# Half of x transposed on VectorE and moved inside SBUF, instead of on TensorE

## The chip, the core and the metric

The kernel runs on one core of a Trainium2 chip. A core has five engines with their own instruction streams: TensorE (PE in the profile, with PEld for its weight loads), VectorE (DVE), ScalarE (ACT), GpSimd (POOL) and SyncE (SP). SP only issues transfers here; ACT and POOL can issue transfers too. Engines work out of SBUF (128 partitions), matmuls write into PSUM (8 banks), and 16 transfer engines move data between device memory (DRAM) and SBUF or inside SBUF. The metric is device time of one execution in microseconds (us).

## The reference: what is computed

The input x is 2048 rows (positions) of 512 features, in bf16. Two branches are computed from it and mixed by a gate per row:

```python
g = sigmoid((x * gate_w).sum(-1, keepdims=True))
X = rfft2(x) * (w_r + 1j * w_i);  a = irfft2(X)            # spectral branch
h = x @ w1 + b1;  act = h * tanh(softplus(h));  b = act @ w2   # dense branch, 512 -> 1792 -> 512
out = g * a + (1 - g) * b
```

## The kernel before, in words

**Data.** x lies in SBUF as 16 tiles `xo[:, t, :]` of 128 rows by 512 features. Both branches need the features on the partitions, so x is also kept transposed, as `xT`: four groups `q` of 128 features by 2048 rows. A row tile `t` is 128 columns of it. Even and odd features are separated, which is why the transposes read with a step of two elements.

**Transposes.** The loop at L466 makes ten groups of TensorE transposes, `tr0a` to `tr14` (L476, 64 matmuls of 128 columns, two tiles per full group), each followed by an eviction `evx` from PSUM to `xT` by VectorE (L404, 1024 elements per partition for a full group; ScalarE may take the four half groups).

**Spectral branch.** The sequence of 2048 positions is split into 16 by 128, and the transforms are matmuls with small tables. In order:
- For each quarter `h` of the rows, VectorE forms the sum `ts` and the difference `td` of the two halves of the features in `xT` (L497, helper line L409). Steps `a1` (L512) transform them, ScalarE copies one part (`eg`, L519) and VectorE combines (`e1p`, `e1m`, `e1f`).
- `s1` (L538) transforms the other axis, `e2` evicts, and SP writes 16 pieces to a DRAM scratch (`r1w`, L546). When all are there, four transfers read them back in another order (`r1r`, L619).
- `s2` (L635) completes the forward transform with the table `RF` (`ld_rf`). VectorE multiplies with the filters W (`wm`, 16 instructions, helper line L409), GpSimd combines the products (`wz`, 16 instructions). The edge columns of W are handled apart: `wcols` (GpSimd), `rcw` (TensorE, L584 and L585), `weff` (VectorE), `wab1` and `wab2` (GpSimd, L598 to L605), and small steps `cv`, `crv`, `cm`, `chs`, `wc` per pair.
- `s2i` (L695) begins the inverse transform; `e4` evicts, and a second exchange through DRAM follows (`r2w`, `r2r`).
- For each row tile: `s1i` (L723), eviction `e5`, `a1i` (L734), `gc` on ScalarE, `sam` and `sap` on VectorE (L745, both scale by the gate), `sbm` and `sbp` on GpSimd (three of the 32 on VectorE; L751, helper line L409), which give the spectral share in `ga`.

**Dense branch.** In four quarters `c` of 512 rows: `mm1` (L773, 14 groups of four matmuls with 512 columns; the first four groups of the first quarter are cut into halves), `mish` on ScalarE (L788) into `act[:, c % 3]`, and `mm2` (L803, per row tile two half groups of seven matmuls). The result is scaled by 1 - g in `bev` (L755 on ScalarE or L756 on VectorE), and `sum` on VectorE (helper line L409) adds the spectral share in `xo`. The last two tiles take one instruction `fin` (L815) in place of both. SP stores pairs of tiles.

**Gate.** `gdot` (L554, VectorE) is one dot product per tile; `gpow` (L559, GpSimd) and three small VectorE steps give g and 1 - g. In the kernel before, the dot products 8 to 15 come after the last `e1`.

**Order.** Every engine and queue runs its list strictly in order. The lists come from one string, `ORDER` (L258): it names all steps in one sequence, with the engine where there is a choice and the PSUM bank. Waits between engines are semaphores derived from what each step reads and writes. So a step that is late holds up everything behind it in its own engine's list.

SP's list begins with the loads of x, part of w1 and the tables FM and GM, then `ld_gw`, 18 loads of W, `ld_rf`, both halves of w2, then the 16 writes `r1w`, the reads `r1r` and `ld_ri`. Three loads of w1 are on ACT's queue. GpSimd issues one small transfer, `ld_b1`.

Of the kernel before, what the change touches and what calls it, by code (L numbers as in the profile page):

```python
# [13 lines left out]
NT = 16  # L14
# [151 lines left out]
class _Graph:  # L166
# [92 lines left out]
    "0M0N0U047050P060O07080Q2z09000S0A010R0B0C0D0T020E0F030V0G0H0W0I0J0X0x60z50Y0yv0Z0K10v1146v212v1H30a1366l51I6q0"  # L259
    "14v0L7011Jv6m6n6w1Kv0b716o0c726p731L40d1M36r1N0e1W50f6s6t741Ov1V70g1560h1Pv1X6x0i6y6u16v7510j1Qa1Zv6z0k1701av1"  # L260
    "971Yv77318v761R41Av781B61Sv7920l0m0n7B01fv7A0o7D10p7C1gv0q1D70r1Cv7E1h30s1r42j1s61j7F20t21v0u1Ev7H00v22v1i17G1"
    "T7J31kv7I1U1lv2451F27K7L01mv1t1Gv2371uv7N47M1vv252Ov7O7b127v1wa2D37c2k28a26v7d07f22Nv7e2l1b67g1n42m2E11ca7h22F"
    "7j01d1ov1e7i1x62Hv7k1p342922Gv1ya1q7l52Av2Ia2Q41z2P17m2Z67n0202n2R2b2B2J22Tv7o2a72C2Sv7p12Ka2Uv2cv7r67q2dv2L2V"
    "27s2M2ev7t02Wv2f67u7v12o2X2ga2p7x52Y7w2h2q7z07y2i2r816802s8F1822t3578H48G362u398J28I373A8L58K2v3B8N63C388M0w8P"
    "18O2w8R28Q2x8T02y8S3D4308U3E63Mv8V38X13Nv8W8Y3Rv3Pg313F7P03G323Qv3Og7Q333H3Tg3Z33Sg7Ra3a13b8Z63iv3I57S08a3mv3J"
    "3jv7T3K3L3U3nv3kg3V47Ua7V33c3Xa3Wv3d3pg3Y3e03v43f3og3w644v7W3lg3x3y49v7Y13g7Xv3z3h3q45v7Z48v46g4028307aa4147g3"
    "r4843ta4Bg3sv4Ag3u4H485a4I24Qv86642434J4K4C4Uv4L874Rv89188a4Vv4Sg4D44Wg4M38b24Ea4N4Fa4Tg8c8A4G4Xg8d74O8Ba4P4Y8"
    "C08e4Z28f14av4ba8D8g4c8t18Ev8v28u8x08w4d8z18y4e9124f904g933929549497096992989B79A4h39C4p59D04qv4ia4x64r59E4yv4"
    "j75534s5D45L156a5Ev5T04z65Ma8h24u504t4k5Uv4wg5N14m5F34vg525V55O8i4l9fv5G5Q4ng515b78k04og8jv5W5P54g5I5Sg5H5768l"
    "5ca9ev5853g9g599F75Rg5A8mv5Kg9H49G5Y5Cg5d65X9J09I9hv5e9lv5j45r39K5Jg8n75sv5ka5Bg9kv5g5z35ag9m6745f5l568a5t19iv"  # L270
    "8o60v5m5hg9j5u5o5ig5v6908pa6F45n5Zg6135w8q26Ga5qg629nv6A645pg8r6B9ov635xg9p6C6N46V59qv6Oa9L78sv5yg6Wa66g6P69rv"
    "6X46Q6H26Eg6d09s6Y9M6S6I6Dg6R6ea6K65g6J9O19Nv6Ug6a6Mg6Z9P9uv9tv6cv9v6f56Tg9Qa9R46bv6g9xv6h6Lg9S6i9wv6kv9y9V06j"
    "g9T9U9Y29W9b79X9Z9a9c9d"
)
NBF = 14
GD_N = 8
# [15 lines left out]
def _build(nc, A_x, A_w_r, A_w_i, B_x, B_w1, B_b1, B_w2, gate_w, out):  # L292
# [8 lines left out]
    with es:  # L301
# [4 lines left out]
        xT = sb("xT", [128, 4, NT * 128], BF)  # L306
# [42 lines left out]
        junk = Tg[:, 6144:6656]  # L349
# [4 lines left out]
        psf = ps[:].rearrange("p b x -> p (b x)")  # L354

# [110 lines left out]
        for t0, h in ((0, 0), (0, 1), (2, 0), (2, 1), (4, None), (6, None), (8, None), (10, None), (12, None), (14, None)):  # L466
# [4 lines left out]
            def f_tr(e, t0=t0, c0=c0, nc_=nc_, pt=pt):  # L471
                ins = None
                for i in range(2):
# [6 lines left out]
            evict(f"evx{t0}" + ("" if h is None else "ab"[h]), 256 * nc_, lambda t0=t0, c0=c0, nc_=nc_: xT[:, c0:c0 + nc_, 128 * t0:128 * (t0 + 2)],  # L480
                  lambda pt=pt, nc_=nc_: psb[:, pt.bank, 0:256 * nc_].rearrange("p (c j) -> p c j", c=nc_), rate=2.0,
                  reads=[("ptr", t0, h)], writes=[("xT", t0 + i, q) for i in range(2) for q in hs], frees=[pt], engs=("dve",) if h is None else ("dve", "act"))
        pb = _Ps(SPEC[::-1])
# [7 lines left out]
        for t in range(NT):  # L491
            if t % 4 == 0:
                G.cur_prio = PR["sp"] + 0.9
                h = t // 4
                cols = slice(512 * h, 512 * h + 512)
                for (nm, o, op) in (("s", 0, ALU.add), ("d", 2, ALU.subtract)):
                    tt(f"t{nm}{h}", lambda o=o, hb=h % 2: Tb[:, hb, o:o + 2, :], lambda cols=cols: xT[:, 0:2, cols],  # L497
                       lambda cols=cols: xT[:, 2:4, cols], op, 1024, rate=2.0,
                       reads=[("xT", 4 * h + i, q) for i in range(4) for q in range(2)], writes=[("T", h % 2, nm)])
            if t % 2 == 0:  # L500
# [3 lines left out]
                for half in range(2):  # L504
# [11 lines left out]
                    pe(f"a1{half}_{t}", 4 * mm(128), f_a1, reads=[("T", hb, "s"), ("T", hb, "d"), "FD"], writes=[("pa", t, half)], alloc=pa,  # L516
# [34 lines left out]
        for t in range(NT):  # L551
            G.cur_prio = PR["gate"] if t >= GD_N else 60.0
            G.add(f"gdot{t}", "dve", dve_dur(512),
                  lambda e, t=t: e.scalar_tensor_tensor(out=junk, in0=xo[:, t, :], scalar=1.0, in1=gwb,  # L554
                                                        op0=ALU.mult, op1=ALU.mult, accum_out=gdot[:, t:t + 1]),
                  reads=[("x", t), "gw"], writes=[("gd", t), "junk"], lock=True, deps=e1s[14] if t >= GD_N else ())

# [206 lines left out]
        for c in range(NCH):  # L764
            hb = c % 3
            G.cur_prio = PR["mm1"] - c
            for ft in range(NFT):
                pd = _Ps(DENSE[c])

                def f_mm1(e, c=c, ft=ft, pd=pd, cols=(0, 512), ks=range(4)):  # L770
                    ins = None
                    for i in ks:
                        ins = e.matmul(ps[:, pd.bank, cols[0]:cols[1]], w1_sb[:, i, 128 * ft:128 * (ft + 1)], xT[:, i, 512 * c + cols[0]:512 * c + cols[1]],  # L773
# [10 lines left out]
                else:  # L784
                    pe(f"mm1_{c}_{ft}", 4 * mm(512), f_mm1, reads=[("xT", 4 * c + i, q) for i in range(4) for q in range(2)] + [("w1", ft, 0), ("w1", ft, 1)],
                       writes=[("pm", c, ft)], alloc=pd, deps=mm2s.get(c - 3, ()), prio=pr_m)
                G.add(f"mish_{c}_{ft}", "act", act_dur(512, True),
                      lambda e, ft=ft, pd=pd, hb=hb: e.activation(act[:, hb, ft, :], ps[:, pd.bank, :], AF.Mish, bias=b1f[:, ft:ft + 1]),  # L788
                      reads=[("pm", c, ft), "b1f"], writes=[("act", hb, ft)], frees=[pd], prio=PR["mish"])
# [148 lines left out]
```

## Time and profile before

| | |
|---|---|
| Median of 3 runs | 130.04 us (129.64 to 130.09) |
| Span of the profiled execution | 128.0 us |
| The same less the median | -2.04 us |
| PE busy | 124.4 us (97%) |
| DVE busy | 92.2 us (72%) |
| ACT busy | 68.9 us (54%) |
| POOL busy | 54.4 us (42%) |
| Chain that ended last, by engine | PE 94%, transfers 3% |
| Moved | 20.11 MB, mean 157 GB/s |

The profile shows one execution; its own time is known only as its span, from the first to the last instruction. Lines are those of the kernel before (L773 is line 773); where a helper records an operation, its line stands for several steps. In a row of the costliest groups, the last number is the idle time of the engine just before these instructions, with what ended most of it. In the chain, each piece has a start, a length and what worked in it. A row of transfers gives the median time from issue to landing.

### The profile page before, as it was taken

To read this page: it belongs to the slowest core of one execution; us is meant where nothing else is said; L and a number is where in the kernel's file an instruction comes from. 1 tells how busy PE (TensorE), PEld (TensorE's weight loads), DVE (VectorE), ACT (ScalarE), POOL (GpSimd) and SP (SyncE) were. 2 spreads that over 40 slices of the span, in tenths; PEclk is the share of its full clock that TensorE was granted. 3 is DMA by queue.
4 is the path that set the end of the run, shared out by engine and by line. 5 is a ranking of instruction groups with operands and counts; after the bars stand their busy time and mean duration, and the time that the engine had idled before them with its cause. 6 is when DMAs were issued, how large, how long until landed. Compare 5 with 4: busy or idle time off the path is not lost.

```text
span 128.0 us, 2725 instructions
## 1 busy us (share of the span) xinstructions
PE 124.4 (97%) x1046; PEld 67.9 (53%) x1046; DVE 92.2 (72%) x176; ACT 68.9 (54%) x113; POOL 54.4 (42%) x82
## 2 busy tenths in 40 slices
PE   7899999999999999999999999999999999999992
PEld 5698566545444444444444444444674457464482
DVE  0359997999989929998957900500399799999872
ACT  1339377889978784224024274487873475462300
POOL 4000000001000996979688394000038986998120
DMA  3999999999976398002304105449600204022231
GB/s 76 346 390 394 303 185 185 173 272 354 334 235 202 99 384 356 0 0 61 108 0 133 38 0 164 133 104 351 239 0 5 82 0 164 3 87 82 82 123 41
DMA packets 18653, 20.11 MB, mean 157 GB/s; under 512 B 1488, under 2 KB 15696, under 8 KB 18512
## 3 DMA queue, kind: packets, MB, share of 16 engines
q1 hardware_dynamic: 17792, 19.15, 49.7%
q10 hardware_dynamic: 816, 0.79, 1.9%
q8 instruction: 8, 0.13, 0.5%
q14 instruction: 5, 0.04, 0.1%
q0 software_dynamic: 32, 0.00, 0.0%
HBM read 13.64 MB, written 6.29 MB: 156 GB/s over the span
## 4 chain that ended last, share of the span: by engine, by line
PE 94%; DMA 3%; SPq 0%; DVE 0%; issue 0%
PE ps L803 38%; PE ps L773 38%; DMA xo<-in_A_x_dram 3%; PE ps L734 3%; PE ps L723 3%; PE ps L512 3%; PE ps L538 3%; PE ps L476 3%; PE ps L695 2%; PE ps L635 2%; SPq L374 0%; DVE xo L815 0%; PE ps L652 0%; PE ps L484 0%; PE ps L425 0%
## 5 line engine op out<-in xcount | busy, mean ns | idle before, releaser
L773 PE MATMUL ps<-xT,w_sb 128*128 128x512 bf16 (+1 forms) x240 | 52.9, 365 | 0.0
L803 PE MATMUL ps<-w_sb,act 128*128 128x512 bf16 (+2 forms) x252 | 51.6, 355 | 0.0
L788 ACT ACTIVATE act<-ps,b1f 128x512 bf16<-128x512 f32 x56 | 38.4, 688 | 18.5 <-PE ps L773 17.3
L803 PEld LDWEIGHTS ps<-w_sb,act 128*128 128x128 bf16 x252 | 22.7, 98 | 22.3 <-issue 0.8
L773 PEld LDWEIGHTS ps<-xT,w_sb 128*128 128x128 bf16 x240 | 22.3, 98 | 21.2 <-issue 0.6
L409 POOL TENSOR_TENSOR Tg<-Qb 128x256 bf16<-128x256 f32 x29 | 22.1, 790 | 21.9 <-DVE Qb L745 21.8
L409 POOL TENSOR_TENSOR Zb<-Qb 128x510 bf16<-128x510 f32 x16 | 19.8, 1268 | 5.1 <-DVE Qb L409 5.0
L409 DVE TENSOR_TENSOR Qb<-ps,WT 128x1024 f32<-128x1024 f32 x16 | 18.8, 1213 | 3.4 <-PE ps L635 3.4
L755 ACT ACTIVATE xo<-ps,omg 128x512 bf16<-128x512 f32 x8 | 5.5, 687 | 18.4 <-PE ps L803 10.1
L745 DVE SCALAR_TENSOR_TENSOR Qb<-ps,gcol,Qb 128x256 f32<-128x256 f32 x32 | 13.7, 475 | 1.5 <-ACT Qb L739 1.0
L404 DVE CAST Ybuf<-ps 128x1024 bf16<-128x1024 f32 x7 | 8.6, 1222 | 7.1 <-PE ps L695 6.7
L409 DVE TENSOR_TENSOR Abuf<-ps,Tg 128x512 bf16<-128x512 f32 x16 | 10.4, 685 | 2.4 <-PE ps L512 2.1
L576 POOL COPY wrv<-WT 128x32 bf16<-128x32 bf16 x2 | 0.4, 223 | 26.1 <-DMA WT<-in_A_w_i_dram 26.1
L405 ACT ACTIVATE Ybuf<-ps 128x1024 bf16<-128x1024 f32 x9 | 9.1, 1021 | 4.3 <-PE ps L695 4.3
L554 DVE SCALAR_TENSOR_TENSOR Tg<-xo,Tg 128x512 bf16<-128x512 bf16 x16 | 11.0, 688 | 0.3
L404 DVE CAST Zb<-ps 128x512 bf16<-128x512 f32 x6 | 4.1, 687 | 8.9 <-PE ps L723 8.9
L404 DVE COPY xT<-ps 128x1024 bf16<-128x1024 bf16 (+1 forms) x10 | 5.6, 579 | 5.4 <-PE ps L476 5.4
L409 DVE TENSOR_TENSOR xo<-xo,Tg 128x512 bf16<-128x512 bf16 x14 | 8.5, 615 | 0.3 <-ACT xo L755 0.3
L739 ACT ACTIVATE Qb<-ps,gcol 128x256 f32<-128x256 f32 x16 | 7.0, 475 | 2.7 <-PE ps L734 1.6
L405 ACT ACTIVATE Zb<-ps 128x512 bf16<-128x512 f32 x10 | 5.7, 596 | 4.6 <-PE ps L723 3.2
L598 POOL TENSOR_TENSOR ch<-wq 128x32 f32<-128x32 f32 x1 | 0.6, 624 | 12.5 <-DVE wq L593 12.5
L476 PE MATMUL ps<-ident,xo 128*128 128x128 bf16 x64 | 5.1, 225 | 0.5 <-DMA xo<-in_A_x_dram 0.5
(59 smaller groups left out, 92.8 us busy)
## 6 DMA issues: line engine op xcount, KB each, us to landing
Abuf<-scr SPq DMA_DIRECT2D x8, 512.0 KB, 5.4
scr<-Ybuf SPq DMA_DIRECT2D x16, 128.0 KB, 3.9
scr<-Ybuf SPq DMA_DIRECT2D x4, 512.0 KB, 3.8
w_sb<-in_B_w_dram SPq DMA_DIRECT2D x2, 896.0 KB, 13.6
out_dram<-xo SPq DMA_DIRECT2D x7, 256.0 KB, 2.0
xo<-in_A_x_dram SPq DMA_DIRECT2D x3, 512.0 KB, 7.7
rt<-c_rt SPq DMA_DIRECT2D x2, 512.0 KB, 8.5
WT<-in_A_w_r_dram SPq DMA_DIRECT2D x7, 128.5 KB, 10.4
```

What stands on the lines that cost most here:

```text
L404: fs = {"dve": ("dve", dve_dur(n, rate=rate), lambda e: e.tensor_copy(out=dst(), in_=src())), "act": ("act", act_dur(n), lambda e: e.activ ...
L405: "act": ("act", act_dur(n), lambda e: e.activation(dst(), src(), AF.Copy))}
L409: f = lambda e: e.tensor_tensor(out=o(), in0=i0(), in1=i1(), op=op)
L476: ins = e.transpose(psb[:, pt.bank, o:o + 128], xo[:, t0 + i, d0:d0 + 255:2], ident[:, :])
L512: ins = e.matmul(ps[:, pa.bank, 256 * i:256 * i + 256].rearrange("p (s m) -> p s m", s=4)[:, r:4 - r:3 - 2 * r, :], Tb[:, hb, 2 * r + half ...
L554: lambda e, t=t: e.scalar_tensor_tensor(out=junk, in0=xo[:, t, :], scalar=1.0, in1=gwb, op0=ALU.mult, op1=ALU.mult, accum_out=gdot[:, t:t ...
L739: lambda e, t=t, sl=sl, p5=p5: e.activation(gC[:, sl, :].rearrange("p (i n) -> p i n", i=2), ps[:, p5.bank, :].rearrange("p (i n) -> p i n ...
L745: lambda e, t=t, sl=sl, p5=p5, o=o, op=op: e.scalar_tensor_tensor(out=st1[:, sl, o::2, :], in0=ps[:, p5.bank, :].rearrange("p (i n) -> p i ...
L755: G.add_multi(f"bev_{t}", [("act", act_dur(512, True), lambda e: e.activation(xo[:, t, :], ps[:, pd.bank, :], AF.Copy, scale=omg[:, t:t + ...
L773: ins = e.matmul(ps[:, pd.bank, cols[0]:cols[1]], w1_sb[:, i, 128 * ft:128 * (ft + 1)], xT[:, i, 512 * c + cols[0]:512 * c + cols[1]], sta ...
L788: lambda e, ft=ft, pd=pd, hb=hb: e.activation(act[:, hb, ft, :], ps[:, pd.bank, :], AF.Mish, bias=b1f[:, ft:ft + 1]),
L803: ins = e.matmul(ps[:, pd.bank, cs_], act[:, hb, ft, 128 * tl:128 * (tl + 1)], w2_sb[:, ft, cs_], start=(ft == 0), stop=(ft == NFT - 1))
```

## The change

- The groups `tr8`, `tr10`, `tr12` and `tr14` (32 of the 64 transposes) and their four evictions are gone.
- In their place VectorE transposes the eight tiles 8 to 15 (`tp8` to `tp15`), each as blocks of 32 by 32, into a scratch area that lies in the third part of `act`.
- A block transpose stays within 32 partitions. So sixteen transfers inside SBUF (`sh00` to `sh33`), of 32 partitions by 1024 elements (64 KB) each, bring the blocks to their partitions in the second half of `xT`. Each of them waits for all eight `tp`. Eight are issued by GpSimd and eight by SP.
- The second half of `xT` has another order of columns: 32 rows from each of four groups lie together. The `mm1` groups of the third and fourth quarter, their `mish` and the sums `ts2`, `td2`, `ts3`, `td3` read it with matching patterns; these sums become eight of half the size and wait for all sixteen transfers. So do the `mm1` groups of these quarters.
- `mish` of the third quarter also waits until the scratch area in `act` has been read.
- The dot products of the gate get two scratch rows in turn, and those of tiles 8 to 15 no longer wait for the last `e1`.
- `ORDER` is a new sequence for all engines. SP's list is the same up to the first load of W; then come its eight transfers, and behind them one half of w2 and the other loads of W, the other half of w2 and `ld_rf`, mixed with the writes `r1w`. On GpSimd the eight transfers stand ahead of `gpow` and `wcols`. On TensorE eleven `mm1` groups of the third quarter and four half groups of `mm2` (tiles 3 and 4) now precede `rcw` and `s2_0`, where one group did; and 21 half groups of `mm2` precede the first `s1i`, where 16 did. More `mm2` tiles are evicted by ScalarE.

```diff
-GD_N = 8
+SHQ = ("pool", "sp", "pool", "sp")
...
-        xT = sb("xT", [128, 4, NT * 128], BF)
+        xT = sb("xT", [128, 8192], BF)
...
-        junk = Tg[:, 6144:6656]
+        junk = (Tg[:, 6144:6656], Tg[:, 7168:7680])
...
+        xTp = xT[:, 0:4096].rearrange("p (q s) -> p q s", q=4)
+        xTb = xT[:, 4096:8192].rearrange("p (a q t j) -> p q a t j", a=4, q=4, t=8)
+        Zb32 = act[:, 2].rearrange("p f s -> p (f s)")[:, 0:4096]
+        Zw = Zb32.rearrange("p (b h e t j) -> p t h b e j", b=4, h=2, e=2, t=8)
...
-        for t0, h in ((0, 0), (0, 1), (2, 0), (2, 1), (4, None), (6, None), (8, None), (10, None), (12, None), (14, None)):
+        for t0, h in ((0, 0), (0, 1), (2, 0), (2, 1), (4, None), (6, None)):
...
+        for t in range(8, NT):
+            G.add(f"tp{t}", "dve", dve_dur(512), lambda e, t=t: e.transpose(
+                Zw[:, t - 8], xo[:, t, :].rearrange("p (b j e) -> p b e j", b=8, e=2)),
+                reads=[("x", t)], writes=[("Z", t)])
+        shs = []
+        for b in range(4):
+            for a in range(4):
+                shs.append(dma(f"sh{b}{a}", xT[32 * b:32 * b + 32, 4096 + 1024 * a:5120 + 1024 * a], Zb32[32 * a:32 * a + 32, 1024 * b:1024 * b + 1024],
+                               reads=[("Z", t) for t in range(8, NT)], writes=[("xB", b, a)], nbytes=65536, queue=SHQ[b], tail=1.9, bw=250e3))
+        XB = [("xB", b, a) for b in range(4) for a in range(4)]
...
+                    for e_ in range(2):
+                        xs = [xTb[:, e_ + 2 * i, :, 4 * h - 8:4 * h - 4, :] for i in range(2)]
+                        tt(f"t{nm}{h}{e_}", lambda o=o, e_=e_, hb=h % 2: Tb[:, hb, o + e_, :].rearrange("p (t a j) -> p a t j", t=4, a=4),
+                           lambda xs=xs: xs[0], lambda xs=xs: xs[1], op, 512, rate=2.0,
+                           reads=XB, writes=[("T", h % 2, nm, e_)])
...
-            G.cur_prio = PR["gate"] if t >= GD_N else 60.0
+            G.cur_prio = PR["gate"]
...
-                  reads=[("x", t), "gw"], writes=[("gd", t), "junk"], lock=True, deps=e1s[14] if t >= GD_N else ())
+                  reads=[("x", t), "gw"], writes=[("gd", t), ("junk", t % 2)], lock=True)
...
-                        ins = e.matmul(ps[:, pd.bank, cols[0]:cols[1]], w1_sb[:, i, 128 * ft:128 * (ft + 1)], xT[:, i, 512 * c + cols[0]:512 * c + cols[1]],
+                        o = ps[:, pd.bank, cols[0]:cols[1]]
+                        ins = e.matmul(o if c < 2 else o.rearrange("p (a t j) -> p a t j", a=4, t=4), w1_sb[:, i, 128 * ft:128 * (ft + 1)],
+                                       xTp[:, i, 512 * c + cols[0]:512 * c + cols[1]] if c < 2 else xTb[:, i, :, 4 * c - 8:4 * c - 4, :],
```

55 lines of the change are left out of this document (30 added, 25 removed).

## The prediction

> **What bounds the kernel now.** I read the page's busy table and its slices first, then the chain of waits in order of time, then the idle times by line, and last the table by stretch for the final stage. The busy shares and the slices, each digit a fortieth of the span (3.2 us):
>
> ```profile
> PE 124.4 (97%) x1046; PEld 67.9 (53%) x1046; DVE 92.2 (72%) x176; ACT 68.9 (54%) x113; POOL 54.4 (42%) x82
> ...
> DVE  0359997999989929998957900500399799999872
> ```
>
> PE leads. VectorE has two full stretches, about 10 to 45 us and 93 to 126 us. The chain (start, length, what) says whether PE ever waits:
>
> ```profile
> 5.57 0.40 PE ps L476 x4
> ...
> 12.16 0.89 PE ps L476 x16
> 13.06 0.86 PE ps L773 x4
> ...
> 41.29 0.01 PE ps L585
> ...
> 79.14 0.57 PE ps L695 x32
> ...
> 90.83 0.45 PE ps L723 x8
> ...
> 93.93 1.51 PE ps L803 x7
> ...
> 125.69 0.02 issue
> 125.71 0.35 DVE xo L815
> ```
>
> From 5.57 to 125.69 the chain is PE work without a hole, so TensorE's own work is the time, and what is left after it is one small VectorE instruction and a store. This execution spans 128.0 us, 2.04 below the median 130.04 of the runs; I keep that distance and work with differences. The last stage is less one-sided than the chain makes it look. The busy time from 90.80 to 126.10, and the two kinds of instruction in which VectorE and GpSimd meet there (ns min/median/max):
>
> ```profile
> sum 35.30, PE 34.87 PEld 21.07 DVE 30.76 ACT 16.27 POOL 22.08; mean PE 8.72 PEld 5.27 DVE 7.69 ACT 4.07 POOL 5.52
> ```
> ```profile
> L409 DVE TENSOR_TENSOR xo<-xo,Tg x14: 411/512/965, 96.5 to 121.3; 128x512 bf16<-128x512 bf16 x14
> ```
> ```profile
> L409 POOL TENSOR_TENSOR Tg<-Qb x29: 720/727/964, 94.8 to 121.5; 128x256 bf16<-128x256 f32 x29
> ```
>
> VectorE works 30.76 of 35.30 us there. Whatever makes this stage begin later meets VectorE as the next bound. This is where I expect the gain to go.
>
> **What goes from TensorE.** 32 of the 64 transposes go (groups tr8 to tr14). Sixteen take 0.89 us on the chain, so 32 take 1.78. They lie on the path, so that is the whole gain on offer. The L773 matmuls of the third and fourth quarter keep their number but now read runs of 128 elements instead of 512. The transposes of L476 read every second element and take 0.0556 per 128 columns; L773, which reads densely, takes 0.86/16 = 0.054. I price the change at nothing; if all of that 0.0016 were due to the step, the 448 pieces of 128 columns would cost 0.7. The Mish activations read the same elements in another order, beside TensorE; also nothing.
>
> **What comes to VectorE.** Eight transposes of 128x512 bf16 come, four evictions of 128x1024 go, and the four sums and differences of halves 2 and 3 become eight of 512. No row is a VectorE transpose. The near rows, and three forms of the last stage that I need further down (busy us, mean ns of one, idle before):
>
> ```profile
> L554 DVE SCALAR_TENSOR_TENSOR Tg<-xo,Tg x16: 680/691/693, 17.3 to 44.6; 128x512 bf16<-128x512 bf16 x16
> L554 DVE DVE_READ_ACCUMULATOR Tg<-xo,Tg x16: 80/82/90, 17.9 to 45.2; 128x1 f32 x16
> ```
> ```profile
> L404 DVE CAST Zb<-ps 128x512 bf16<-128x512 f32 x6 | 4.1, 687 | 8.9 <-PE ps L723 8.9
> L756 DVE TENSOR_SCALAR xo<-ps,omg 128x512 bf16<-128x512 f32 x6 | 4.5, 746 | 1.2 <-PE ps L803 1.2
> L815 DVE SCALAR_TENSOR_TENSOR xo<-ps,omg,Tg 128x128 bf16<-128x128 f32 (+2 forms) x4 | 1.9, 484 | 1.5 <-PE ps L803 1.5
> L409 DVE TENSOR_TENSOR Qb<-ps,WT 128x1024 f32<-128x1024 f32 x16 | 18.8, 1213 | 3.4 <-PE ps L635 3.4
> L409 DVE TENSOR_TENSOR Abuf<-ps,Tg 128x512 bf16<-128x512 f32 x16 | 10.4, 685 | 2.4 <-PE ps L512 2.1
> L404 DVE COPY xT<-ps 128x1024 bf16<-128x1024 bf16 (+1 forms) x10 | 5.6, 579 | 5.4 <-PE ps L476 5.4
> L409 DVE TENSOR_TENSOR Tg<-xT 128x1024 bf16<-128x1024 bf16 x8 | 5.3, 683 | 0.0
> ```
>
> Below stands 0.34 (half of the 683 for 1024 elements, the doubled rate), above 1.21 (1024 elements at the single rate). I take 0.69, because 512 elements from and to SBUF is the row of L554. The halved sums lie between 0.34 and 0.69; I take 0.4, the doubled rate with a fixed part.
>
> The transposes need tiles 8 to 15. Those loads, and what a transfer costs the two queues:
>
> ```profile
> L374 SPq DMA_DIRECT2D xo<-in_A_x_dram x1: 432/432/432, 3.7 to 3.7; - x1
> ...
> DMA to landing us min/median/max: 7.7/7.7/7.7
> ```
> ```profile
> L374 SPq DMA_DIRECT2D xo<-in_A_x_dram x1: 777/777/777, 5.5 to 5.5; - x1
> ...
> DMA to landing us min/median/max: 9.5/9.5/9.5
> ```
> ```profile
> L374 POOL DMA_DIRECT2D braw<-in_B_b_dram x1 | 0.8, 785 | 0.8 <-POOLq L923 0.8
> ```
> ```profile
> scr<-Ybuf SPq DMA_DIRECT2D x16, 128.0 KB, 3.9
> ...
> out_dram<-xo SPq DMA_DIRECT2D x1, 64.0 KB, 1.5
> ...
> braw<-in_B_b_dram POOLq DMA_DIRECT2D x1, 3.5 KB, 4.4
> ```
>
> Tiles 8 to 11 are there at 3.7 + 7.7 = 11.4, tiles 12 to 15 at 15.0. In VectorE's new order four transposes and the eviction evx4 (0.66, the full-size form within the mean of 0.579) fill 11.4 to 14.8, the other four 15.0 to 17.8. The four evictions that go were 2.6 us of VectorE, the transposes are 5.5, all of it ahead of the race below. So all sixteen transfers start at 17.8.
>
> **The race at 28 us.** GpSimd issues eight of them, 0.785 each: the last starts at 17.9 + 7 x 0.785 = 23.4. Landing takes 1.5 (64 KB in a quiet queue) to 4.4 (GpSimd's own under load). I take 3.9, the row that starts in SBUF under load: all is there at 27.3. SP's eight (0.43 each, like the smaller row of x) are issued by 21.2 and land by 25.1. Between 17.8 and the first halved sum VectorE has two sums (0.68), seven instructions of the 685 form (0.65 each by 10.4/16), five dot products (0.77 with their read) and a small copy: 9.9, ready at 27.7. So the transfers are hidden by 0.4. That holds up to 0.84 per transfer on GpSimd, since (27.7 - 3.9 - 17.9)/7 = 0.84; from there each us of lateness is a us of the kernel.
> TensorE reaches a10_8, the first that needs them, at 5.6 plus 24 transposes (1.3), 22 groups of L773 (four matmuls, 0.86 each: 19.0), eight a1 steps (four matmuls of 128 columns, 0.22 each) and two s1 steps (two of 512, 0.43 each) = 28.6. It needs the third halved sum: 27.7 + 1.2 = 28.9. Then a11_8, one group later, needs the seventh: 30.5 against 30.0. I put 0.7 us of TensorE waiting here.
>
> **The loads behind.** SP's queue now holds 17 of the 18 loads of W, both of w2 and a table behind the transfers, and mixes them with the writes of the first exchange:
>
> ```profile
> L374 SPq DMA_DIRECT2D WT<-in_A_w_r_dram x9: 582/610/652, 7.5 to 12.8; - x9
> ```
> ```profile
> L374 SPq DMA_DIRECT2D scr<-Ybuf x20: 359/616/4219, 23.5 to 81.0; - x20
> ```
> ```profile
> POOL wrv L576 <- DMA WT<-in_A_w_i_dram: 26.1, 1, 26.1
> ```
> ```profile
> Abuf<-scr SPq DMA_DIRECT2D x8, 512.0 KB, 5.4
> ```
>
> From 21.2 ten loads of W and one of w2 (0.61 each) take SP to 27.9. Then r1w0b waits for e2_0, which VectorE does after the halved sums, about 32, and all loads queued behind it wait with it. Sixteen writes (0.616), seven loads of W, one of w2 and the table are issued by 47.3; the first read back lands 5.4 later, at 52.7. On GpSimd's queue wcols, which idled 26.1 us for W before, stands behind the eight transfers and the gates' power. TensorE needs W's edge columns and that read for rcw and s2_0. Their place was 41.29; ten groups of L773 and four half groups of L803 (seven matmuls, 1.51) have moved ahead, 41.29 + 8.6 + 6.0 - 1.78 + 0.7 = 54.8. So a cover of 2.1 us hides what W and the exchange lose; without the moved groups their place would be 40.2, and 12.5 us would stand on the path. Two POOL steps are no longer early: the power for the gates and the seven wab instructions stand right in front of the first product:
>
> ```profile
> L605 POOL TENSOR_SCALAR wab<-ch 128x16 f32<-128x16 f32 (+1 forms) x7 | 3.0, 455 | 0.1
> L559 POOL TENSOR_TENSOR gcol<-omg,gdot 128x16 f32<-128x16 f32 x1 | 2.9, 2942 | 0.0
> L409 POOL TENSOR_TENSOR Zb<-Qb 128x510 bf16<-128x510 f32 x16 | 19.8, 1268 | 5.1 <-DVE Qb L409 5.0
> ```
>
> From 55, with 3.0 for wab, about 1 for the two instructions ahead of it (the 455 ns form twice) and 19.8 for the products, GpSimd is at 78.8; sixteen small instructions between them take from nothing to 7.3 (455 ns each), so it is through at 78.8 to 86.1, and I take 85, because the products also wait for VectorE (5.1 us before). The last s2i needs it; it was at 79.14 and has seven groups of L773 and one half group of L803 more ahead: 79.14 + 6.0 + 1.5 - 1.78 + 0.7 = 85.6. I put 0.3 of waiting here, where the upper end gives 0.5. TensorE then ends at 125.69 - 1.78 + 0.7 + 0.3 = 124.9.
>
> **The last stage.** In the new order 21 half groups of L803, not 16, precede the first s1i (52 groups of L773 in both): 90.83 + 5 x 1.51 - 1.78 + 1.0 = 97.6. VectorE's part begins at 98.0. Of its 30.76 us three evictions of L756 (0.75 each) and two of the e5 form (0.69) have gone to ScalarE: 27.1 remain, 125.1 without one gap. Before there were 4.5 us of gaps, 1.5 of them while waiting for TensorE at the very end; I keep 1.2. And GpSimd's 22.08 us now fill the same, shorter stage without a pause. A final sum takes 0.41 at best and 0.965 at worst; the mean is 0.61, and those over the minimum average about 0.72. If all fourteen did, VectorE would lose 1.5; I take 0.8. The last VectorE instruction ends at 98.0 + 27.1 + 1.2 + 0.8 = 127.1 against 126.06, so +1.0: 131.1 us.
> The Trainium skill, "SBUF — State Buffer", section "Who interferes with whom", says that a VectorE instruction with two SBUF inputs and a GpSimd instruction that reads SBUF lock one port pair against each other, the loser waiting in full. The trace agrees with its 0.41 to 0.965 for one shape; by the rule each sum could wait out a whole GpSimd instruction, an estimate that only lengthens the same term.
>
> **Rivals.** First, faster: TensorE still sets the end. That needs the waits at 28 and 85 us and the gaps of the last stage to come out small, under 0.2 in all for the gaps plus contention: VectorE's gapless 125.1 is then level with TensorE's 124.9 + 0.35. The time is 128.9 to 129.3, at the very best 130.04 - 1.78 = 128.3. For it: TensorE is the chain now. Against: 30.76 of 35.30.
> Second, GpSimd's transfers are late. The one row, of 14 partitions, gives 0.785; these have 32 on either side and run beside SP's loads. At 1.2 us each the data are there at 30.2, so +2.5 on top: 133.6; at 1.5 it is 135.7.
> Third, a VectorE transpose costs 1.21. Then the first four and evx4 end at 16.9, the others at 21.8, all behind is 4.0 later: 135.1. The rows for it are only those of four-byte data. The Trainium skill, "VectorE: DVE Perf Modes", section "The three transpose paths", gives 311 ns for 128x128 bf16; four of these would be an estimate of 1.24, while no run here shows one.
> Fourth, the loads of W or the read back miss 54.8: with 2.1 of cover, a phase of loads 4 us longer gives +1.9: 133.0. The gates' power, 2.9 us on GpSimd after the last dot product, decides here too, if it ends after 54.
>
> **How the numbers follow.** A VectorE-bound last stage with the transfers about in time: 0.37, of which 0.20 stays within 0.5%. TensorE-bound and faster 0.28, late transfers on GpSimd's queue 0.19, slow transposes 0.07, late W 0.09. About 0.5% (0.65 us) is what a measurement of this kernel can tell from no change. That makes faster 0.28, same 0.20, slower 0.52. The likeliest case alone spans 129.8 to 132.3. The range reaches down to the faster case's middle, 128.7, and up into the late transfers, 134.8; beyond lie the slow transposes and the rest of the first and second rival.
>
> **What would show it.** Right: L476 with 32 matmuls; eight VectorE transposes near 0.69 us, done near 17.8; the last GpSimd transfer landing at 27 to 28; under 1 us of idle TensorE before L512 near 29; the first L723 matmul near 97.6; a chain that ends in VectorE and GpSimd instead of TensorE; final sums with a mean above 0.65 us. Wrong: a TensorE hole of over 2 us near 29 (second or third rival, told apart by when the transposes end), a hole before L635 near 55 (fourth), or a chain of TensorE to the end with the last L803 at 124 to 125 (first).

## The result, and the profile after

The changed kernel takes 131.51 us (median of 4 runs, 131.12 to 132.11) beside 129.91 us of the kernel before on the same chip (129.64 to 130.09): a ratio of 1.0138, 95% interval 1.0103 to 1.0172. That is 1.6 us slower. The prediction was 131.1. The profiled execution spans 129.7 us, before 128.0. Where some runs of a kernel lie more than 1.5% above its fastest one, a ratio is that of the faster runs alone.

The page after: busy times, VectorE's slices, and the chain that ended last by engine (before, it was TensorE's alone from 5.57 us to the end).

```profile
PE 123.0 (95%) x1014; PEld 66.1 (51%) x1014; DVE 91.6 (71%) x178; ACT 69.4 (54%) x119; POOL 56.3 (43%) x90
...
DVE  0456999898699981179499795541006997999992
...
PE 85%; DMA 5%; DVE 3%; POOL 2%; issue 1%; POOLq 1%; DVEq 0%
```

TensorE lost 1.4 us of busy time and is no longer the whole chain. The chain in order of time (start, length, what) shows the two places where it leaves TensorE:

```profile
45.20 3.19 PE ps L795 x15
48.40 6.87 DMA Abuf<-scr
55.31 0.63 PE ps L656 x32
...
86.13 0.57 PE ps L716 x32
...
97.82 0.89 PE ps L744 x16
...
117.53 1.51 PE ps L830 x7
...
119.32 1.66 DVE Qb L766 x4
121.05 1.71 POOL Tg L414 x2
123.00 0.87 POOLq L900
123.87 0.88 POOL Tg L414
124.95 0.72 DVE xo L842
...
126.75 0.52 DVE xo L842 x2
```

The first is the read back of the first exchange (issued 48.40, landed 55.27; before, issued 42.26). The second is the end: from 119.3 us on VectorE (L766, L842) and GpSimd (L414) hand work to each other, while TensorE's last matmul ends at 119.10 + 6.28 = 125.38. The rows of the changed part, with the longest wait of TensorE (in all, times, longest):

```profile
L489 DVE STREAM_TRANSPOSE act<-xo x8: 667/669/711, 12.1 to 16.9; 128x512 bf16<-128x512 bf16 x8
```
```profile
L379 POOL DMA_DIRECT2D xT<-act x8: 496/496/549, 17.8 to 21.3; - x8
...
DMA to landing us min/median/max: 2.0/2.4/2.5
```
```profile
L414 DVE TENSOR_TENSOR Tg<-xT x8: 414/415/419, 26.6 to 30.9; 128x512 bf16<-128x512 bf16 x8
```
```profile
PE ps L656 <- DMA Abuf<-scr: 1.2, 1, 1.2
```

The transposes are through at 17.6, GpSimd's transfers have landed by 24.4, and VectorE comes to the first halved sum at 26.6: nothing waits there. TensorE waits 1.23 us in front of L656, near 55. Last, the stage from the first L744 to VectorE's last instruction, and the two kinds of instruction that meet in it:

```profile
sum 29.50, PE 27.55 PEld 17.66 DVE 27.83 ACT 18.07 POOL 22.63; mean PE 27.55 PEld 17.66 DVE 27.83 ACT 18.07 POOL 22.63
```
```profile
L414 DVE TENSOR_TENSOR xo<-xo,Tg x14: 406/572/947, 105.9 to 126.3; 128x512 bf16<-128x512 bf16 x14
```
```profile
L414 POOL TENSOR_TENSOR Tg<-Qb x29: 719/837/917, 101.4 to 124.7; 128x256 bf16<-128x256 f32 x29
```

VectorE is busy for 27.83 of 29.50 us, and both medians have risen: the sums from 512 to 572 ns, GpSimd's additions from 727 to 837 ns.

### The profile page after: what moved, and what is told of

The parts are those of the page before. It is cut to its first block, busy times and chain, and to the rows that moved or that the text cites. A ratio compares the mean times of both kernels' runs of the same rounds, so it can differ in the third digit from the quotient of the medians.

```text
span 129.7 us, 2726 instructions
## 1 busy us (share of the span) xinstructions
PE 123.0 (95%) x1014; PEld 66.1 (51%) x1014; DVE 91.6 (71%) x178; ACT 69.4 (54%) x119; POOL 56.3 (43%) x90
## 4 chain that ended last, share of the span: by engine, by line
PE 85%; DMA 5%; DVE 3%; POOL 2%; issue 1%; POOLq 1%; DVEq 0%
PE ps L795 37%; PE ps L830 29%; DMA Abuf<-scr 5%; PE ps L744 3%; PE ps L755 3%; PE ps L533 3%; PE ps L559 3%; PE ps L430 3%; POOL Tg L414 2%; PE ps L656 2%; PE ps L716 2%; DVE Qb L766 1%; PE ps L481 1%; DVE xo L842 1%; DVE xT L409 1%
## 5 line engine op out<-in xcount | busy, mean ns | idle before, releaser
L795 PE MATMUL ps<-xT,w_sb 128*128 128x512 bf16 (+1 forms) x240 | 53.8, 365 | 0.3 <-DVE xT L409 0.3
L830 PE MATMUL ps<-w_sb,act 128*128 128x512 bf16 (+2 forms) x252 | 52.2, 355 | 0.0
L811 ACT ACTIVATE act<-ps,b1f 128x512 bf16<-128x512 f32 x56 | 36.5, 687 | 26.6 <-PE ps L795 26.6
L795 PEld LDWEIGHTS ps<-xT,w_sb 128*128 128x128 bf16 x240 | 22.3, 98 | 21.9 <-DVE xT L409 0.8
L414 POOL TENSOR_TENSOR Tg<-Qb 128x256 bf16<-128x256 f32 x29 | 22.6, 812 | 17.4 <-DVE Qb L766 17.4
L414 POOL TENSOR_TENSOR Zb<-Qb 128x510 bf16<-128x510 f32 x16 | 20.0, 1268 | 3.2 <-DVE Qb L414 2.6
L414 DVE TENSOR_TENSOR Qb<-ps,WT 128x1024 f32<-128x1024 f32 x16 | 18.9, 1215 | 3.4 <-PE ps L656 3.3
L766 DVE SCALAR_TENSOR_TENSOR Qb<-ps,gcol,Qb 128x256 f32<-128x256 f32 x32 | 13.6, 473 | 1.5 <-issue 0.8
L580 POOL TENSOR_TENSOR gcol<-omg,gdot 128x16 f32<-128x16 f32 x1 | 2.9, 2942 | 26.6 <-DVE Tg L575 26.6
L410 ACT ACTIVATE Ybuf<-ps 128x1024 bf16<-128x1024 f32 x9 | 9.1, 1024 | 6.5 <-PE ps L716 6.2
L414 DVE TENSOR_TENSOR Abuf<-ps,Tg 128x512 bf16<-128x512 f32 x16 | 10.4, 685 | 2.7 <-ACT Tg L540 1.5
L379 POOL DMA_DIRECT2D xT<-act x8 | 4.0, 503 | 15.5 <-DVE act L489 15.5
L575 DVE SCALAR_TENSOR_TENSOR Tg<-xo,Tg 128x512 bf16<-128x512 bf16 x16 | 10.5, 685 | 0.2
L776 ACT ACTIVATE xo<-ps,omg 128x512 bf16<-128x512 f32 x11 | 7.3, 687 | 5.2 <-PE ps L830 3.5
L777 DVE TENSOR_SCALAR xo<-ps,omg 128x512 bf16<-128x512 f32 x3 | 2.3, 751 | 10.8 <-PE ps L830 10.8
L414 DVE TENSOR_TENSOR xo<-xo,Tg 128x512 bf16<-128x512 bf16 x14 | 9.0, 653 | 0.0
L540 ACT ACTIVATE Tg<-ps 128x512 f32<-128x512 f32 x8 | 4.7, 594 | 6.2 <-PE ps L533 6.2
L410 ACT ACTIVATE Zb<-ps 128x512 bf16<-128x512 f32 x12 | 7.0, 603 | 1.0 <-PE ps L744 1.0
L409 DVE COPY xT<-ps 128x512 bf16<-128x512 bf16 (+1 forms) x6 | 2.9, 505 | 5.7 <-PE ps L481 5.7
## 6 DMA issues: line engine op xcount, KB each, us to landing
scr<-Ybuf SPq DMA_DIRECT2D x16, 128.0 KB, 2.2
```

The lines of the kernel that those rows point to most:

```text
L379: t = G.add(name, queue, issue if issue != 0.62 or queue != "pool" else 1.0, lambda e: e.dma_start(dst, src), reads=reads, writes=writes, ...
L409: fs = {"dve": ("dve", dve_dur(n, rate=rate), lambda e: e.tensor_copy(out=dst(), in_=src())), "act": ("act", act_dur(n), lambda e: e.activ ...
L410: "act": ("act", act_dur(n), lambda e: e.activation(dst(), src(), AF.Copy))}
L414: f = lambda e: e.tensor_tensor(out=o(), in0=i0(), in1=i1(), op=op)
L540: G.add(f"eg_{t}", "act", act_dur(512), lambda e, gb=gb, pa=pas[0], pv=pv: e.activation(G0[:, gb].rearrange("p t c (m s) -> p t c m s", s= ...
L575: lambda e, t=t: e.scalar_tensor_tensor(out=junk[t % 2], in0=xo[:, t, :], scalar=1.0, in1=gwb, op0=ALU.mult, op1=ALU.mult, accum_out=gdot[ ...
```

## The experiments

Theory A was that of the prediction with one correction from the trace: VectorE and GpSimd set the end of the last stage, and the 1.23 us before L656 shift its beginning. The rivals were that TensorE still sets the end and its wait is all of the loss, and that VectorE and GpSimd slowing each other means nothing. All times are medians beside the kernel before on the same chip, which measured 129.75 to 129.81 in these comparisons.

**TensorE's last tile cut, after and before.** Every second product of the last tile is left out (the flag that marks the last product of a sum moves with it and is not shown), so TensorE ends earlier and nothing else changes:

```diff
-                        for ft in fts:
+                        for ft in (fts if t < NT - 1 else fts[::2]):
```

> The changed kernel with every second of the 42 products of the last tile of L830 left out (part of the computation is missing): TensorE ends 1.5 us earlier, near 123.9 in the trace, all else is the same. Theory A (VectorE and GpSimd set the end of the last stage): same time, 131.3 to 131.6. Rival (TensorE still sets the end, its later start being the loss): 130.0.

> The kernel before with the same products of the last tile left out (part of the computation is missing). Theory A (there TensorE is the bound to the end): 128.4 to 128.8, 1.2 to 1.5 us less than before. Rival (VectorE's last stage was already level with TensorE there, so that the change could gain nothing): no more than 0.5 us less, 129.5.

Changed kernel: 131.02 us, ratio 1.0095 (1.0076 to 1.0113). Kernel before: 128.83, ratio 0.9925 (0.9902 to 0.9948). The last matmuls (start, length) and VectorE's last instructions of the changed kernel with the cut, from the timeline:

```profile
118.71 4.73 PE L830 MATMUL ps<-w_sb,act 128*128 128x512 bf16 x35
...
126.28 0.60 DVE L842 SCALAR_TENSOR_TENSOR xo<-ps,omg,Tg 128x128 bf16<-128x128 f32 x2
```

TensorE ends at 123.44, 1.9 us earlier, and VectorE's last instruction only 0.4 earlier, at 126.88. Those 0.4 are not from the cut: the wait before L656 happened to be 0.67 in this execution instead of 1.23. In the kernel before, TensorE ends 0.38 us before VectorE does; with the cut the kernel takes 0.97 us less, TensorE ends at 124.40 instead of 125.68, and the chain is still TensorE's up to the last VectorE instruction. So after the change TensorE no longer sets the end, and before it did. The expected time of the first run was missed by 0.3 for the wait; the second gained 0.97 where 1.2 to 1.5 were expected.

**GpSimd's additions halved, after and before.** A test of VectorE and GpSimd in the last stage; VectorE's instructions stay, and a memset is put in on GpSimd ahead of the stage:

```diff
-lambda o=o: o, lambda sl=sl: st1[:, sl, 0:2, :], ...
+lambda o=o, n=128 if t >= 14 else 64: o[:, :, 0:n], lambda sl=sl, n=...: st1[:, sl, 0:2, 0:n], ...
```

> The changed kernel with GpSimd's additions of the last stage (L414 Tg<-Qb) on half of their columns (part of the computation is missing); a memset of 2,048 columns of Tg comes into GpSimd's idle time near 42 us so that the other columns hold numbers. VectorE's instructions are untouched. Theory A with contention (VectorE's sums wait for GpSimd's instructions): the mean of VectorE's final sums falls from 0.65 to near 0.5, its last instruction ends 1 to 1.5 us earlier, 130.0 to 130.5. Rival (VectorE's own instructions fill the stage, GpSimd takes nothing from them): the mean stays at 0.62 to 0.66 and the time within 0.4 of 131.5.

> The control to the run with half additions: the same cut (GpSimd's additions of the last stage on half of their columns, one memset of Tg ahead; part of the computation is missing) in the kernel before. Theory A (before, TensorE ends the stage and VectorE and GpSimd have room): within 0.4 us of before, 129.4 to 130.0, and a chain of TensorE to the end. Rival (the port contention costs the same in both kernels, and says nothing of the change): 128.0 to 128.4.

Changed kernel: 129.60 us, ratio 0.9983 (0.9970 to 0.9996), below the expected 130.0 to 130.5. Kernel before: 130.15, ratio 1.0029 (1.0016 to 1.0041). The changed kernel's sums, and its stage from the first L744 (96.80) to VectorE's end:

```profile
L414 DVE TENSOR_TENSOR xo<-xo,Tg x14: 405/414/942, 105.0 to 123.8; 128x512 bf16<-128x512 bf16 x14
```
```profile
sum 28.00, PE 27.59 PEld 17.75 DVE 25.48 ACT 18.10 POOL 14.46; mean PE 27.59 PEld 17.75 DVE 25.48 ACT 18.10 POOL 14.46
```

The sums' median falls from 572 to 414 ns without any change to them, VectorE's busy time by 2.35 us, and the stage from 29.5 to 28.0, where TensorE ends it (its last matmul at 124.42, VectorE at 124.80). Against the changed kernel this is 1.9 us; 0.9 of it may be the wait before L656, which was 0.35 here. In the kernel before the same cut shortens the sums as well (median 416), and its stage stays at 35.2 us. It is even 0.34 us slower: the memset stands ahead of GpSimd's first product there, which starts at 51.14 instead of 50.21, and between 48 and 54 the chain runs through VectorE's products. Sums that are slower beside GpSimd's instructions exist in both kernels; they cost time only where VectorE and GpSimd set the end. Whether the shorter sums of VectorE or the shorter GpSimd part of the chain did more was not separated.

**The loads ahead of the exchange.** SP's order alone:

```diff
+        q = order["sp"]
+        at = [t.name for t in q].index("r1w0b")
+        late = [t for t in q[at:] if t.name.startswith("ld_") and t.name != "ld_ri"]
+        order["sp"] = q[:at] + late + [t for t in q[at:] if t not in late]
```

> The changed kernel with the order of SP's queue altered in one place: the loads of W, of w2 and the forward table, which stand between and behind the writes of the first exchange, all stand ahead of its first write. Theory A (the wait of 1.2 us before L656 near 55 us is the cover of the loads that ran out, and what it costs shifts everything behind it): the first read back lands before TensorE reaches L656 at 54.1, no wait there, first L744 near 96.6 instead of 97.8, 130.3 us. Rival B (the read back is late because the last eviction of the exchange is late, not because of the loads): the wait stays above 0.8 us and the time at 131.5. Rival C (the wait goes, but the last stage has its own bound and does not move with it): no wait before L656 and still 131.2 to 131.6.

131.00 us, ratio 1.0084 (1.0057 to 1.0111), where 130.3 was expected. L656 starts at 54.02 without a wait, as theory A had it. The four transfers of the first read back, in the changed kernel and here:

```profile
L379 SPq DMA_DIRECT2D Abuf<-scr x4: 344/592/763, 48.4 to 50.1; - x4
...
DMA to landing us min/median/max: 6.9/8.3/9.3
```
```profile
L379 SPq DMA_DIRECT2D Abuf<-scr x4: 338/429/432, 49.0 to 50.3; - x4
...
DMA to landing us min/median/max: 3.9/5.6/7.9
```

The read is issued no earlier than in the changed kernel, but it lands 3 us sooner. So what this order gains is not an earlier issue, since the loads now hold up the writes instead, but a sooner landing: in the changed kernel two pieces of W and the table are issued right ahead of the read, from 45.9 to 47.8. Still, the first L744 is at 97.19, not at the expected 96.6, because the chain now runs through the second exchange:

```profile
84.83 0.62 PE ps L716 x32
...
85.48 1.24 DVE Ybuf L409
...
86.73 4.95 DMA scr<-Ybuf
...
92.32 4.83 DMA Abuf<-scr
...
97.19 1.07 PE ps L744 x16
```

From the start of the last L716 step to the first L744 it takes 12.4 us: eviction, write, issue, read. In the changed kernel TensorE had 97.82 - 86.13 = 11.7 us of work in that place and the data came in just before it was done (first read back issued at 93.1, 4.0 to landing at the least). So half of the 1.23 us came back (0.6 in the trace, 0.5 in the medians), and the second read back took the rest.

**The way of the tiles later.** One memset on GpSimd between the last transpose and its first transfer:

```diff
+        ms = _Task("ms", "pool", 4.0, lambda e: e.memset(Qf[:, 0:5120], 0.0))
+        ms.deps = [by[f"tp{t}"] for t in range(8, NT)]
...
+        q.insert([t.name for t in q].index("sh21"), ms)
```

> The changed kernel with one memset of 5,120 columns of Qb (not in use then) on GpSimd between VectorE's last transpose and GpSimd's first transfer: 4.5 us by the 1.80 us of the memset of 2,048 columns in the run with half additions. GpSimd's last transfer then starts near 25.8 and lands near 28.2, VectorE would have been ready for it at 26.6. Theory of the prediction (beyond the slack each us of lateness is a us of the kernel): 1.6 us of waiting, 133.1; TensorE idle 1.3 to 2 us near 29. Rival (the way of the tiles has more room, TensorE's work in between absorbs it): 131.5, no idle TensorE near 29.

139.22 us, ratio 1.0715 (1.0667 to 1.0762): 7.7 us more than the changed kernel, where 1.6 were expected. The memset took 4.37 us. GpSimd's landings, and the table by stretch (busy times, then the granted clock, which is TensorE's clock as a share of full speed, then DMA share and GB/s):

```profile
L379 POOL DMA_DIRECT2D xT<-act x8: 496/496/549, 22.0 to 25.5; - x8
...
DMA to landing us min/median/max: 2.2/7.0/7.6
```
```profile
30.00:32.00 2.00, 0.00 (x0) 0.00 (x0) 0.00 (x0) 0.00 (x0) 0.00 (x0) 1.00 1.32 229
...
34.00:36.00 2.00, 1.57 (x7) 0.77 (x8) 2.00 (x7) 1.18 (x2) 0.00 (x0) 0.50 0.30 66
...
40.00:42.00 2.00, 2.00 (x17) 1.16 (x16) 0.65 (x2) 1.54 (x3) 0.00 (x0) 1.00 0.91 280
```

Two things add to the delay. GpSimd's transfers now run beside SP's loads of w2 and W (issued from 22.7 on) and land in 7.0 instead of 2.4 us, so the last is there at about 33, and TensorE idles 5.4 us near 29. And when it goes on, its clock is at half: from 34 to 36 the granted clock is 0.50, four matmuls of L795 take 1.87 us instead of 0.86, and it is back at 1.00 only at 40. From 34.2 to 39.9 some 5.5 us of work at half speed lose about 2.7 us; with the 5.4 of idleness that is 8.1. In exchange the wait of 1.23 before L656 is gone, and two small waits of 0.3 each, on ScalarE and before L744, are new: 7.5, against the 7.7 measured.

**Loads ahead of the transfers.** SP waits 4.8 us for the transposes; eight loads (half of w2 and seven of W, not eight of W as the expectation says) were put there, the rest ahead of the exchange:

```diff
+        q = order["sp"]
+        at = [t.name for t in q].index("sh12")
+        late = [t for t in q[at:] if t.name.startswith("ld_") and t.name != "ld_ri"]
+        rest = [t for t in q[at:] if t not in late]
+        order["sp"] = q[:at] + late[:8] + rest[:8] + late[8:] + rest[8:]
```

> The changed kernel with SP's queue altered in two places: eight loads of W go ahead of SP's eight transfers, into the time in which SP waits for the transposes (12.8 to 17.6), and the other loads of W, w2 and the table ahead of the first write of the first exchange. SP then issues the writes of the exchange without loads in between. Theory A (the read back was late because of the loads): no wait before L656, as in the run in which all loads go ahead of the writes, where a wait for the second read back took its place before L744; 130.7 to 131.1. The second exchange is not touched, so nothing more is expected. Rival (the transfers of SP come later behind the loads): a wait near 29 us and 131.5 or more.

The four runs took 131.78, 132.50, 134.32 and 134.52 us; the ratio, that of the two faster ones, is 1.0185 (1.0142 to 1.0228). All four lie above the expected 130.7 to 131.1. The profile is that of the longest. There the rival came true, as the landing of GpSimd's transfers shows, and TensorE's first steps that need them (in brackets the idle time before):

```profile
DMA to landing us min/median/max: 7.2/7.4/7.5
```
```profile
30.92 0.40 PE L533 MATMUL ps<-FMs,Tg 128*128 128x128 bf16 x4 [2.07 <-DVE Tg L414]
31.81 1.86 PE L795 MATMUL ps<-xT,w_sb 128*128 128x512 bf16 x4 [0.49 <-issue]
```

The transfers are issued when they were in the changed kernel, at 17.7 to 21.2, and land 5 us later, because the loads are in the queues ahead of them. A pause of 2.07 us, four short matmuls and 0.49 us more were followed by the half clock here (four matmuls in 1.86 us). The mean granted clock was 0.979 in the two longer runs and 0.994 and 0.992 in the two faster ones, so the half clock most likely did not come in these; no trace of them was kept. That the change puts nearly all loads of W and w2 behind the transfers is thus not a detail of the queue: a landing of 2.3 to 2.4 us on GpSimd's queue was seen only in the runs that keep it so.

**The change without its new order.** The transposes, transfers and halved sums in the order of the kernel before (`tp8` to `tp15` and the transfers behind `evx6`; the string `ORDER` is not shown), all transfers on GpSimd:

```diff
-SHQ = ("pool", "sp", "pool", "sp")
+SHQ = ("pool", "pool", "pool", "pool")
```

> The change without its new order: VectorE's transposes (right behind the eviction evx6), the sixteen transfers (all on GpSimd's queue) and the halved sums, everything else in the order and on the engines of the kernel before, the loads of W, w2 and the table ahead of the exchange as there. Theory A (the new order hides the way of tiles 8 to 15 behind the work of the second quarter and pays for it at the end): TensorE reaches a1 of tile 8 near 20 us, the transposes are done at 18 and the data there at 28.5, so it waits 8 to 9 us; the end is then TensorE's again: 130 - 1.8 + 8.5 = 136.7, between 134.5 and 139. Rival (the move itself is nearly free and the new order is what costs): 130 to 132.

147.28 us, ratio 1.1350 (1.1320 to 1.1379): 10 us more than expected. TensorE idles 4.3 us near 17 and 10.0 us near 26, and it works at a granted clock of 0.50 from 21.6 to 25.0 and from 36.2 to 42. The transfers land in 8.0 to 9.1 us here. So the pauses are 14.4 us instead of 8.5, and 9.2 us of work at half speed lose another 4.6: 130 - 1.8 + 14.4 + 4.6 = 147.2. The new order is what makes the move bearable; the direction was as theory A had it and the size was not, for the same two reasons as in the two runs above.

**What was on offer.** In the kernel before, 28 of the 32 transposes of tiles 8 to 15 on TensorE were left out:

```diff
-                for i in range(2):
-                    for c in range(c0, c0 + nc_):
+                for i in range(2 if t0 < 8 else 1):
+                    for c in range(c0, c0 + (nc_ if t0 < 8 else 1)):
...
```

> The kernel before with 28 of the 32 TensorE transposes of tiles 8 to 15 left out (of each group of eight one stands, and the eviction copies its 128 columns eight times; part of the computation is missing). VectorE, the queues and the order are as before. Theory of the prediction (what goes from TensorE lies on the path in full): 28 x 0.0556 = 1.56 us less than before, 128.2 to 128.5. Rival (VectorE's last stage is already level with TensorE's, so that a part of the gain was never on offer): 0.2 to 0.8 us less, and a chain that ends in VectorE and GpSimd.

128.77 us, ratio 0.9924 (0.9900 to 0.9949): 1.03 us less, of 1.56 us of matmuls. The chain is still TensorE's to the end, so neither theory is right in full. In the trace 0.33 us went to a wait that the transposes had covered (the L513 step near 17.1, L512 of the kernel before, takes 1.00 instead of 0.67 us), and 0.44 us were lost before 7.1 us, ahead of the transposes that are left out; the second has nothing to do with the cut, and the profiled execution is the longest of the four.

**Another order for the changed kernel.** The lists were drawn up anew from the durations of the trace, once for the changed kernel and once, as a control, for the kernel before. The places that decided:

```diff
-act: ld_w1_0_0 ld_w1_0_1 ld_w1_4_1 table eg_2 eg_0 ...
+act: table ld_w1_0_0 ld_w1_0_1 ld_w1_4_1 mish_0_3 ...
```

> The changed kernel with the same operations, and each engine's list drawn up anew with the durations of the trace: the transfers still ahead of the loads, all loads of W but three ahead of the last writes of the exchange, the last stage with one eviction and one addition fewer on VectorE (e5_2 to ScalarE, e5_1 back, sbp_14 to GpSimd), seven half groups of L830 arranged otherwise around the second exchange. Theory A (the loss is how the order meets the two read backs and VectorE at the end, not the transposes as such): no wait above 0.5 us at 54 us, TensorE ends near 124.5 and VectorE near 125.5 to 126.5; 129.0 to 130.2. Rival (the second exchange and VectorE's 27 us hold the end whatever the order): 130.8 to 131.5.

> The control to the run with the changed kernel's lists: the kernel before, whose lists are drawn up anew in the same way. TensorE has no hole to lose there: 129.3 to 130.0, within 0.5% of before. If it gains as much as the other one gains over the changed kernel, the gain there says nothing of the change.

142.70 and 145.58 us (ratios 1.0999 and 1.1206). Both failed for one reason: the new lists moved first loads of w1 on ScalarE's queue, in the first behind the load of the activation table, in the control the third of them behind the first Mish steps. TensorE then idles 6.3 us at 5.5 us, and 9.3 us at 14 us. They tell nothing about theory A. But in the profiled execution of the first the granted clock stayed at 1.00 through the pause of 6.3 us and behind it. In the second try the first loads and the stores kept their places, and SP's order is that of the run with the loads ahead of the exchange:

```diff
-dve: ... sam_13 sbp_14 sum_9 ...
+pool: ... sbp_8 sbp_14 sbm_15 ...
```

> The changed kernel with SP's order of the run in which all loads go ahead of the first exchange's writes, and with the lists of TensorE, VectorE, ScalarE and GpSimd behind the first 8 us drawn up anew with the durations of the trace; the first loads and the stores, which the first try had moved, keep their places. Two evictions net and the addition sbp_14 leave VectorE. Theory A (the loss lies in how the order meets the read backs and VectorE's last stage, and can be had back): no wait above 0.5 us near 28 or 54 us, 129.3 to 130.4. Rival (VectorE's and GpSimd's last stage behind the second read back is the floor of this form): 130.6 to 131.2.

131.22 us, ratio 1.0109 (1.0081 to 1.0136): the rival. TensorE has no wait near 28 or 54, and VectorE has lost work (26.52 us busy in its last stage), but GpSimd has gained an addition, and the stage takes 28.9 us. The chain ends over GpSimd:

```profile
120.55 1.62 POOL Tg L464 x2
...
123.62 1.56 POOL Tg L464 x2
```

Relieving VectorE moved the end to GpSimd. No version with the whole computation was found that beats the kernel before.

## Why the prediction came out right, step by step

The stage from the first s1i step (L744 in the changed kernel, L723 before) to the end of VectorE's last instruction, in the profiled executions of runs with the whole computation (us):

| kernel | first s1i | last matmul ends | VectorE ends | stage |
|---|---|---|---|---|
| before | 90.8 | 125.68 | 126.06 | 35.2 |
| change in the old order | 108.3 | 143.18 | 143.57 | 35.2 |
| changed | 97.8 | 125.38 | 127.27 | 29.5 |
| loads ahead of the exchange | 97.2 | 124.94 | 126.83 | 29.6 |
| transfers later | 105.25 | 132.99 | 134.87 | 29.6 |
| loads ahead of the transfers | 100.85 | 128.42 | 130.30 | 29.5 |
| first try of new lists, kernel before | 107.1 | 142.13 | 142.52 | 35.4 |
| first try of new lists, changed | 108.9 | 136.46 | 137.03 | 28.2 |
| second try of new lists | 98.1 | 126.19 | 126.99 | 28.9 |

Where much of TensorE's work is left behind the first s1i, the stage takes 35 us and TensorE ends it, its last matmul 0.38 us ahead of VectorE's last instruction. Where that work has been moved ahead, VectorE and GpSimd need 28 to 29.6 us, whenever the stage begins. This is the likeliest case of the prediction: a start near 97.6 and 27.1 + 1.2 + 0.8 = 29.1 us behind it.

- **The 1.78 us from TensorE**: right as work. Its last matmul ends 0.30 earlier; 1.23 went to the wait before L656 and about 0.3 to one before the first L795 steps. "The whole gain on offer" was too large: in the kernel before, 1.56 us of the same transposes brought 1.03. The price of nothing for the runs of 128 elements held: a matmul takes 365 ns on average in L773 before and in L795 after.
- **VectorE's transposes at 0.69, done at 17.8**: 0.67, done at 17.6. The third rival, 1.21 each, fell. The 311 ns for 128x128 in the Trainium skill's "VectorE: DVE Perf Modes", section "The three transpose paths", had given an estimate of 1.24; the measurement is about half of that.
- **GpSimd's transfers at 0.785 and 3.9 to landing**: mis-sized; they took 0.50 and 2.4. With SP's (0.59 each, landing in at most 2.8) all was there by 24.9, VectorE came at 26.6, and the slack was 1.7 instead of 0.4. So TensorE's 0.7 of waiting near 29 (its two terms, 0.3 and 0.5, add up to 0.8) was nothing. The bounds of 1.5 to 4.4 for the landing held in the changed kernel, but were no bounds: beside or behind loads the same transfers took 7.0 to 9.1.
- **The loads behind, a cover of 2.1, priced at nothing**: this step failed. The read back was issued at 48.40 instead of 47.3 and landed 6.87 later instead of 5.4, at 55.27, and TensorE was there at 54.08, 0.7 earlier than put, since it had not waited at 29. The fourth rival's mechanism came, at 1.2 us instead of 1.9. The run with the loads ahead of the exchange shows that they were its cause, and where: there the read was issued at 48.97, no earlier, and landed in 3.9 instead of 6.87. The step had counted what the loads cost SP in issuing, and had taken the landing from the kernel before, where no load stands right ahead of the read.
- **Last s2i at 85.6, first s1i at 97.6**: 86.13 and 97.82. The places were right by luck, because two errors nearly cancelled: 0.7 and 0.3 of waiting were put elsewhere, 1.23 came at L656. What the step did not see is the second read back: with the first wait gone, L744 could begin only 0.6 us earlier.
- **The last stage**: VectorE busy 27.83 (27.1 put, and 0.8 for contention), gaps 1.67 (1.2 put), end at 127.27 (127.1 put). That sums wait on GpSimd agrees with the Trainium skill's "SBUF — State Buffer", section "Who interferes with whom": the median of a sum fell from 572 to 414 ns when only GpSimd's instructions were halved. The first rival (TensorE sets the end) fell with the cut last tile.
- **From +1.0 to +1.6**: VectorE's end moved by 1.2. The last store was issued at 127.8 instead of 126.1, since the last two instructions of L842 end 0.26 us apart and their stores queue up on SP; that further 0.5 was not in the sum. 0.1 is within the spread of the runs.
- **"Each us of lateness is a us of the kernel"**, the price in the second rival: too cheap, since 5.4 us of idleness, with the half clock behind them, cost 7.7.

## What to carry to other kernels

When work is taken from the bounding engine, look up how long each other engine is busy behind the last point that cannot move (here the second read back) before counting the gain: the fullest second engine of that stage decides. The place of a transfer in the queues is part of its price: the same 64 KB took 2.4 us with no loads around it and three times that beside them. And a pause of a bounding TensorE can cost more than its length: in four traces here the granted clock was at half behind it, in one, after 6.3 us, it was not.

## What the runs showed of the hardware that was not expected

- In four traces the granted clock fell to 0.50 in or after a pause of TensorE: 2.07 us, 0.4 us of work and another 0.49 us of pause (0.50 from 31.5 to 35.0, loads ahead of the transfers); 5.12 us (0.50 from 33.1 to 39.9, transfers later); 4.34 and 10.02 us (old order); 1.99 and 9.28 us (new lists for the kernel before). It stayed at 1.00 at the 1.23 us before L656, and also at 6.34 us in the new lists for the changed kernel, so that the length of the pause alone does not decide it here. The Trainium skill, "TensorE: Matmul & The Clock Gate", section "HAM oscillation — how this bites in real kernels", warns of pauses over about 3.4 us; here less was enough twice, and once more was not.
- Transfers of 64 KB inside SBUF on GpSimd's queue were delayed by loads on SP's queue (2.4 to 7.0 us and more). The Trainium skill, "Trainium Kernel Development and Optimization", section "Key Constraints", says that the queues of all engines run on the same 16 DMA engines and interleave; the traces agree.
- A VectorE transpose of 128x512 bf16 inside SBUF takes 0.67 us, no longer than an elementwise instruction with two bf16 inputs of that size (L575, 0.68).
